# Linear attention into a gated MLP: q loaded in longer runs with kv on both partition halves, and a written order in place of a planner

## The chip, the cores and the metric

One core of a Trainium2 chip. The time is that of one execution on the device in microseconds. A run's time is that of the whole program; the span in a profile goes from the first to the last instruction of the profiled execution. TensorE (PE) multiplies, VectorE (DVE) and ScalarE (ACT) work element by element and empty PSUM, GpSimd (POOL) and SyncE (SP) issue DMAs here. TensorE's operands lie in SBUF, its results in PSUM.

## What is computed

```python
kv  = einsum('bhsd,bhse->bhde', k, v)            # 8 batches, 8 heads, 576 tokens, 64 wide
out = einsum('bhsd,bhde->bhse', q, kv)
x   = out / sqrt(mean(out*out, -1) + 1e-6) * g_norm
x   = x.transpose(0, 2, 1, 3).reshape(4608, 512)  # 4608 tokens, 512 wide
h   = x @ w_in                                    # 512 x 2048
g   = maximum(h, 0) + alpha * minimum(h, 0)
y   = g @ w_out                                   # 2048 x 512, float32 out
```

## The kernel before

Everything is cast to float16 while it is loaded (GpSimd's DMAs cast); PSUM is float32. The 4608 tokens are cut into nine windows `w` of 512. A window goes through three steps, and three windows are under way at a time:

- attention for window `w`: `kv_mm` (name `kv`) makes kv of a batch, 40 matmuls, and `kv_copy` (`kvc`) puts it into `kv_masked` with ScalarE. `rows_mm` (`R.w.1` and `R.w.3`, two token tiles of 128 each) multiplies q, which lies transposed in `qt_sb`, by kv into `or_ps`. Then come squares (`q2`, `q3`), the root (`rs`), the normalisation (`n`, `x_rows`) and a DMA transpose on SyncE into `xt` (`x`).
- the first product: `M.w.u` (and `Ma`) is one block of 128 features, four matmuls, emptied by ScalarE (`r`, `m_sb`) and VectorE (`s`, `gt`). From window 3 on half of it goes by a Strassen-like scheme (`f`, `t`, tiles `mY`, `mV`, `mX`).
- the second product, always by that scheme: `p.w.n.k` is a group of four matmuls into `yX`, `yY`, `yZ`, with sums `S` by VectorE, reads `y` by ScalarE or VectorE, and stores `st`.

q, k and v of batch `b` are loaded two windows ahead by GpSimd (`ld.q.b.t`, `ld.k.b.0`, `ld.v.b.0`; the last 64 tokens apart, as `.4`). k and v come in runs of four tokens of one head, 512 bytes of float16 per partition; 128 partitions times four tokens make the 512 tokens of the main part. From batch 3 on q comes in four loads of 128 tokens, each partition one token of all eight heads, in runs of 64 elements. A DMA transpose (`q.b.t`, line 400) turns each of the four into `qt_sb`. DMA transposes of q and x and some stores (`late`, and `st` of `c12`) share SyncE's queue, which goes in order. A load of k or v must wait until kv of the batch before has been made, a load of q until the old one has been turned. Before each load GpSimd copies one element of `gt` (`gate`, line 1402), which keeps the load from starting early; loads of k and v also copy one element of a transposed tile.

From the second loop on (near 66 us) the order of each engine's work comes from a planner: `AT` holds a due time for each kind of step, and `in_order` takes the due step whose needs are met. The first 66 us have a hand-written order.

Of the kernel before, what the change touches and what calls it, by code (L numbers as in the profile page):

```python
# [17 lines left out]
def kernel(  # L18
# [190 lines left out]
    def load_q(b, t):  # L209
        if (b, "q") not in stages:  # L210
            stages[b, "q"] = stage_for(b, "q", [P, TPP, H, D])
        nc.gpsimd.dma_start(  # L212
            out=stages[b, "q"][:, t, :, :],
            in_=srcs["q"][b, :, t * P : (t + 1) * P, :].rearrange("h p d -> p h d"),
        )
# [176 lines left out]
    def dma_t(b, ts=tuple(range(NT))):  # L392
        qt = qt_sb[b % 2][:, :, PAD : PAD + S]
        for t in ts:
            c0, c1 = t * P, min((t + 1) * P, S)
            if t == TPP:
                src = rem_of(b, "q")[0:REM]
            else:
                src = buf_of(b, "q")[:, t] if b < B_NAT else stages[b, "q"][:, t]
            nc.sync.dma_start_transpose(  # L400
                out=qt[:, :, c0:c1], in_=src.rearrange("p h d -> p (h d)"),
            )
        for j in range(NPAIR):
            qts[b, j] = qt_sb[b % 2][:, j, PAD : PAD + S]

# [99 lines left out]

    def rows_mm(w, tiles):
        o_ps = row_tile([2, 2, NPAIR, D], "or_ps")
        for x, i in enumerate(tiles):
            b, r = divmod(w * W + i * P, S)
            for j in range(NPAIR):  # L510
                if r + P <= S:
                    steps = ((b, PAD + r),)
                else:
                    assert r + PAD == S
                    steps = ((b, S), (b + 1, 0))
                for n, (bb, c) in enumerate(steps):
                    for h in range(2):
                        part = slice(h * D, (h + 1) * D)
                        nc.tensor.matmul(  # L519
                            out=o_ps[:, h, x, j, :],  # L520
                            lhsT=qt_sb[bb % 2][part, j, c : c + P],
                            rhs=kvs[bb, j][part, part],
                            start=(n == 0), stop=(n == len(steps) - 1), skip_group_check=True,
                        )
            ots[w, "r", i] = o_ps[:, :, x]
# [100 lines left out]
    gt_last = []  # L626
    h_turn = [0]
# [72 lines left out]
    def row_pieces(n0):  # L700
        i = 0
        while i < P:
            b, r = divmod(n0 + i, S)
            np_, nt = (P0, T0) if b == 0 else (P, TPP)
            if b < B_NAT and r < np_ * nt:
                t, p = divmod(r, np_)
                cnt = min(P - i, np_ - p)
                yield i, cnt, b, t, p
            else:
                cnt = P - i if b >= B_NAT else min(P - i, S - r)  # L710
                yield i, cnt, None, n0 + i, 0
            i += cnt
# [186 lines left out]
    def quad_out(w, r, h, src, subs=(0, 1)):  # L899
        n0 = w * W + r * HW  # L900
        if n0 >= B_NAT * S and len(subs) == 2:
            put(
                out[n0 : n0 + HW, h * HC : (h + 1) * HC].rearrange("(a p) m -> p a m", p=P),
                src[:],
            )
            return
# [438 lines left out]
    def kv_copy(b):  # L1345
        for i in range(2):
            part = slice(i * D, (i + 1) * D)
            nc.scalar.copy(out=kv_masked[part, b % 4, :, part], in_=kv_tiles[b][part])
# [77 lines left out]
    def load(nm, b):  # L1426
        if nm == "q":
            for t in range(TPP):
                load_q(b, t)
            load_rem(b, "q")  # L1430
        else:
            load_rem(b, nm)
            load_main(b, nm)
# [103 lines left out]
    def put_m2(w):  # L1537
# [17 lines left out]

        full = lambda f, k: f(k) + f(k + 1) if pairs else f(k)
        for k in range(0, 4, 2 if pairs else 1):
            if w > 1:
                sums(3, k, *full(lo, k), *used(7, k))
            sums(1, k, *full(lo, k), *full(hi, k), *used(5, k))  # L1560
            sums(2, k, at(1, k), *used(6, k))
# [105 lines left out]
    def put_rows(w, tiles, free, used):  # L1667
        needs = []
        for i in tiles:
            b, r = divmod(w * W + i * P, S)  # L1670
            needs += [("q", b, t) for t in range(r // P, min((r + P - 1) // P, TPP) + 1)]
            needs.append(("kvc", b))
            if r + P > S:
                needs += [("q", b + 1, 0), ("kvc", b + 1)]
# [16 lines left out]
    def put_moves(w):  # L1691
        b = w + 1
        for t in range(NT if b < B else 0):
            step(("q", b, t), "turn", lambda t=t: dma_t(b, (t,)),
                 (("ld", "q", b, t), *(("R", b - 1, i) for i in (1, 3))))
# [5 lines left out]
    def turned(what, w, i):  # L1701
        if what == "x":
            return xts[w][0:1, 0, i * P : i * P + 1]
        return qt_sb[w % 2][0:1, 0, PAD + i * P : PAD + i * P + 1]
# [7 lines left out]
    def put_load(nm, b):  # L1712
        needs = (("kv", b - 1),) if nm != "q" else ()
        for t in range(NT) if nm == "q" else (TPP, 0):
# [12 lines left out]
            own = (("q", b - 2 if t == TPP else b - 1, t),) if nm == "q" else ()  # L1727
            step(("ld", nm, b, t), "part" if t == TPP else "loadq" if nm == "q" else "load", fn, needs + own + after)

    def put_rest():  # L1730
# [12 lines left out]
        for w in range(min(M1_FROM.values()), NW):  # L1743
            for n in range(1, 5):
# [3 lines left out]
                     (*x_all(w), *((("t", w, n // 2),) if n in (2, 4) else ()), *used))  # L1748
# [24 lines left out]
    for w in range(1, NW):  # L1773
# [3 lines left out]
    LOOP = 27.0  # L1777
    AT = {
# [160 lines left out]
```

## Time and profile before

| | us |
|---|---|
| runs, median of 3 | 273.92 (271.63 to 274.67) |
| the profiled execution | 270.98 |
| its span | 269.2 |
| TensorE busy | 261.9 (97%) |
| VectorE busy | 228.1 (85%) |
| ScalarE busy | 191.8 (71%) |
| GpSimd busy | 94.9 (35%) |

A row of the profile names the line of the kernel, the engine, the operation, and the tiles as written and read (`or_ps<-kv_masked,qt_sb`). Busy time of TensorE contains modelled ends of pipelined matmuls. Engines wait for each other through semaphores; a row's idle time is given with what ended it. "issue" is time in which the profile shows no one to wait for.

### The profile page before, as it was taken

What the parts mean: (1) busy time and instruction counts of PE and PEld (TensorE: products, weight loads), DVE (VectorE), ACT (ScalarE), POOL (GpSimd) and SP (SyncE); (2) the same over time, 40 slices, a digit from 0 to 9 for tenths busy, and PEclk for the clock granted to TensorE, in tenths of its full rate; (3) what the DMA queues carried; (4) which work ended last, traced back from release to release, by engine and by line L of the source; (5) the groups of instructions that cost most, each with busy time, mean ns of one, the idle gap of its engine ahead of it and who ended that gap; (6) DMA issues with size and microseconds to landing.
All of it is one profiled execution on the core that took longest, in us unless ns stands there. A gap on an engine that the chain in (4) does not pass through costs nothing.

```text
span 269.2 us, 6788 instructions
## 1 busy us (share of the span) xinstructions
PE 261.9 (97%) x2477; PEld 182.8 (68%) x2477; DVE 228.1 (85%) x437; ACT 191.8 (71%) x684; POOL 94.9 (35%) x166
## 2 busy tenths in 40 slices
PE   6999999999999999999999999999999999999994
PEld 2554454456556757885788678867885788678883
DVE  6559966899977888999889988998899989978962
ACT  2567637787579779879977997799779983757400
POOL 8853652513530326874346521804040003002100
PEclk9999999999999999999999999999999999999999
DMA  7999999995999899999999993999464013100413
GB/s 189 201 199 206 195 198 189 183 195 92 195 128 169 75 131 126 129 161 197 189 163 156 138 153 66 110 191 129 107 138 99 19 24 119 39 2 11 145 41 118
DMA packets 90821, 35.76 MB, mean 133 GB/s; under 512 B 62996, under 2 KB 88612, under 8 KB 90788
## 3 DMA queue, kind: packets, MB, share of 16 engines
q0 software_dynamic: 57104, 23.68, 68.5%
q1 hardware_dynamic: 32708, 10.63, 24.0%
q10 hardware_dynamic: 976, 1.02, 1.2%
q8 instruction: 19, 0.31, 0.5%
q14 instruction: 14, 0.11, 0.2%
HBM read 36.71 MB, written 9.44 MB: 171 GB/s over the span
## 4 chain that ended last, share of the span: by engine, by line
PE 85%; DMA 8%; ACT 2%; issue 2%; DVE 1%; SPq 1%; POOL 0%; POOLq 0%
PE h_ps L641 23%; PE yY L895 14%; PE yX L895 9%; PE yZ L895 8%; PE mY L1247 8%; PE y L686 5%; PE mV L1247 4%; DMA qt_sb<-qst 3%; PE h_ps L674 2%; DMA vst<-in_v_dram 2%; PE mX L1247 2%; PE or_ps L519 1%; DMA y_sb<-in_g_norm_dram 1%; DMA qst<-in_q_dram 1%; PE kv_ps L1337 1%
## 5 line engine op out<-in xcount | busy, mean ns | idle before, releaser
L641 PE MATMUL h_ps<-xt,w_in_sb 128*128 128x512 f16 x348 | 83.0, 379 | 0.1
L656 DVE SCALAR_TENSOR_TENSOR gt<-m_sb,beta_sb,h_ps 128x512 f16<-128x512 f32 x96 | 67.1, 741 | 4.6 <-ACT m_sb L650 3.6
L650 ACT ACTIVATE m_sb<-h_ps 128x512 f32<-128x512 f32 x96 | 55.0, 604 | 14.3 <-PE h_ps L641 11.9
L641 PEld LDWEIGHTS <-w_in_sb 128*128 128x128 f16 x348 | 33.1, 98 | 32.3 <-issue 0.3
L895 PEld LDWEIGHTS <-s 128*128 128x128 f16 x496 | 48.0, 98 | 8.4 <-DVE s L813 0.2
L895 PEld LDWEIGHTS <-gt 128*128 128x128 f16 x384 | 37.4, 98 | 8.6
L582 ACT ACTIVATE sq_sb<-or_ps 128x64 f16<-128x64 f32 x192 | 39.7, 286 | 2.2 <-PE or_ps L519 2.2
L582 ACT ACTIVATION_READ_ACCUMULATOR sq_sb<-or_ps 128x1 f32 x192 | 39.4, 273 | 0.0
L1402 POOL COPY gate_sb<-gt 1x1 f16<-1x1 f16 x39 | 10.5, 269 | 76.9 <-DVE gt L656 54.7
L895 PE MATMUL yX<-w_out_sb,gt 128*128 128x256 f16 x256 | 35.2, 273 | 0.0
L895 PE MATMUL yY<-wsum,s 128*128 128x256 f16 x256 | 32.9, 273 | 0.0
L698 POOL DMA_DIRECT2D out_dram<-y_sb x24 | 15.2, 639 | 45.8 <-ACT y_sb L957 42.8
L608 DVE TENSOR_TENSOR x_rows<-or_ps,rstd_r 128x512 f16<-128x512 f32 x27 | 17.4, 685 | 9.0 <-ACT rstd_r L592 8.8
L1314 DVE SCALAR_TENSOR_TENSOR gt<-m_sb,beta_sb,mh 128x256 f16<-128x256 f32 x48 | 20.5, 477 | 0.2 <-ACT m_sb L1307 0.2
L1307 ACT ACTIVATE m_sb<-mh 128x512 f32<-128x512 f32 x24 | 15.1, 629 | 6.3 <-DVE mh L1269 6.3
L1266 ACT COPY mu<-mY 128x512 f32<-128x512 f32 x24 | 14.1, 588 | 6.5 <-PE mY L1247 6.5
L1269 DVE TENSOR_TENSOR mh<-mV,mu 128x512 f32<-128x512 f32 x24 | 16.4, 685 | 2.5 <-ACT mu L1266 2.4
L212 POOL DMA_DIRECT2D qst<-in_q_dram x20 | 17.8, 891 | 2.2 <-issue 2.0
L686 PE MATMUL y<-w_out_sb,gt 128*128 128x512 f16 x64 | 16.3, 380 | 0.0
L895 PE MATMUL yZ<-wsum,s 128*128 128x256 f16 x120 | 16.2, 273 | 0.0
L895 PE MATMUL yY<-wsum,gt 128*128 128x256 f16 x128 | 15.5, 273 | 0.0
L1247 PEld LDWEIGHTS <-w_in_sb 128*128 128x128 f16 x144 | 14.1, 98 | 1.6
(150 smaller groups left out, 425.0 us busy)
## 6 DMA issues: line engine op xcount, KB each, us to landing
kst<-in_k_dram POOLq DMA_DIRECT2D x7, 512.0 KB, 7.7
vst<-in_v_dram POOLq DMA_DIRECT2D x6, 512.0 KB, 6.5
out_dram<-y_sb POOLq DMA_DIRECT2D x11, 256.0 KB, 3.2
qst<-in_q_dram POOLq DMA_DIRECT2D x20, 128.0 KB, 4.5
w_out_sb<-in_moe_w_out_dram POOLq DMA_DIRECT2D x8, 256.0 KB, 12.1
out_dram<-y_more POOLq DMA_DIRECT2D x5, 256.0 KB, 4.2
w_in_sb<-in_moe_w_in_dram POOLq DMA_DIRECT2D x2, 512.0 KB, 10.4
qst<-in_q_dram POOLq DMA_DIRECT2D x2, 512.0 KB, 10.7
```

The source lines that it names most:

```text
L212: nc.gpsimd.dma_start(out=stages[b, "q"][:, t, :, :], in_=srcs["q"][b, :, t * P : (t + 1) * P, :].rearrange("h p d -> p h d"),)
L582: nc.scalar.activation(out=sq[:, half, j], in_=o_ps[:, half, j], func=AF.Square, accum_out=ssq[:, half, j : j + 1],)
L608: nc.vector.tensor_tensor(out=xr[:].rearrange("p j h d -> p h j d"), in0=o_ps, in1=rstd[:].unsqueeze(3).to_broadcast([P, 2, NPAIR, D]), op ...
L641: nc.tensor.matmul(out=h_ps[:], lhsT=w_in_blk(c, g), rhs=xts[w][:, c, :], start=(c == 0), stop=(c == NC - 1),)
L650: nc.scalar.activation(out=neg[w, g][:], in_=h_ps[:], func=AF.Relu, scale=-1.0)
L656: nc.vector.scalar_tensor_tensor(out=gts[w, i][:, r, :], in0=neg.pop((w, g))[:], scalar=beta_sb[:, g : g + 1], in1=h_ps[:], op0=ALU.mult, ...
L686: nc.tensor.matmul(out=y[:], lhsT=gt_cols(w, g, a * P, (a + 1) * P), rhs=w_out_blk(g), start=(n == 1), stop=(n == NF),)
L698: engs[store_turn[0] % len(engs)].dma_start(out=dst, in_=src)
L895: nc.tensor.matmul(out=bank, lhsT=lhs, rhs=rhs, start=fresh, stop=(c == NK - 1), skip_group_check=True,)
L1247: nc.tensor.matmul(out=t[bank][:, r, :], lhsT=lhs[:, c, r * P : (r + 1) * P], rhs=rhs[:, c, :], start=(fresh and c == r == 0), stop=(c == ...
L1269: nc.vector.tensor_add(out=h_tile(t, what)[:, :, HW:W], in0=src[:], in1=u[:])
L1314: nc.vector.scalar_tensor_tensor(out=gts[w, i][:, r, cols], in0=m, scalar=beta_sb[:, g : g + 1], in1=h, op0=ALU.mult, op1=ALU.add,)
```

## The change

- From batch 3 on q is loaded like k and v, in two loads of four heads, in 512-byte runs of four tokens. One transpose then holds two heads of all 512 tokens; on its 128 output partitions stand two tokens of a head, 64 partitions each, so a head's tokens lie on either half.
- kv of these batches is therefore kept twice: each head's block lies on both partition halves (one copy of 128x256 and two of 64x256 in place of two of 64x256), and `rows_mm` picks the half by token.
- The tokens of a window stand in another order, with the last 64 of an odd batch first. Tiles that straddle two batches are then made of two pieces of 64 rows, and the output is stored in groups of four tokens.
- The planner is replaced by a list, `ORDER`. `ld.q.5.0@s.3.5` in it is a load that GpSimd gates on the step `s.3.5`; `@!` has no such gate, `@-` the last element made before the list begins.
- Three needs are added for sums whose buffers are read (`read_by`, and one for `t`).

```diff
-    def load_q(b, t):
-        ...
-            out=stages[b, "q"][:, t, :, :],
-            in_=srcs["q"][b, :, t * P : (t + 1) * P, :].rearrange("h p d -> p h d"),
+    QL = 2
+    def load_q(b, i):
+        load_main(b, "q", i * H // QL, (i + 1) * H // QL)
 ...
     def dma_t(b, ts=tuple(range(NT))):
+        for t in ts if b >= B_NAT else ():
+            n = P if t < TPP else REM
+            ...
+                src = stages[b, "q"][:, 2 * t : 2 * t + 2].rearrange("p h t d -> p (h t d)")
+            nc.sync.dma_start_transpose(
+                out=qt_flat(b)[:, t * W : t * W + NC * n].rearrange("p (c n) -> p c n", c=NC),
+                in_=src,
+            )
+    def place_of(b, r):
+        if b >= B_NAT and b % 2:
+            r = r - REM if r >= REM else r + MAIN
+        return divmod(r, P) if r < MAIN else (TPP, r - MAIN)
 ...
+    def row_ops(w, i):
+        ...
+                    half = h if b < B_NAT or t == TPP else t % 2
+                    ...
+                        lhs = qt_flat(b)[part, c : c + n]
+                        rhs = kvs[b][part, half ^ h, j, :]
 ...
     def kv_copy(b):
+        ...
+        nc.scalar.copy(out=kvs[b][:, 0], in_=kv_tiles[b])
         for i in range(2):
-            part = slice(i * D, (i + 1) * D)
-            nc.scalar.copy(out=kv_masked[part, b % 4, :, part], in_=kv_tiles[b][part])
+            part, other = slice(i * D, (i + 1) * D), slice((1 - i) * D, (2 - i) * D)
+            nc.scalar.copy(out=kvs[b][other, 1], in_=kv_tiles[b][part])
 ...
     def put_rows(w, tiles, free, used):
-            needs += [("q", b, t) for t in range(r // P, min((r + P - 1) // P, TPP) + 1)]
+            for b, t, _ in row_parts(w, i):
+                needs += [("q", b, x) for x in ((TPP,) if t == TPP else range(TPP) if b >= B_NAT else (t,))]
 ...
             def fn(t=t, after=after):
-                gate(gt_last[0])
+                for src in load_gate:
+                    gate(src)
 ...
-    LOOP = 27.0
-    AT = {
-        "eyu3": -54736.65, "eyc21": -53910.63, "f2r11": -9714.71, "byu2": -7708.14, "bq23": -7676.19,
-        ...
+    ORDER = """
+        late.2.1 late.2.0 late.2.2 kv.3 M.2.2 S.1.1.0 ld.k.4.4@- S.1.1.1 Ma.2.0 r.2.2 S.1.2.0
+        ...
+        M.2.14 q2.4.0 s.2.15 p.1.3.0 r.2.13 q.4.0 s.2.12 p.2.2.0 ld.q.5.4@s.2.15 q2.4.1 p.2.2.1
+        s.2.13 ld.v.4.4@- p.1.3.1 r.2.14 q.4.3 p.1.3.2 q3.4.1 s.2.14 p.1.3.3 p.2.2.2 q.4.2 S.2.1.1
+        rs.4.1 p.2.2.3 q3.4.0 S.2.3.1 Ma.3.0 y.1.c12 q.4.1 M.3.0 M.3.1 S.2.2.0 y.2.seed r.3.0 n.4.1
+        M.3.2 ld.q.5.1@s.2.12 rs.4.0 S.2.4.0 r.3.1 x.4.1 M.3.3 y.2.c11 n.4.0 st.1.c21 r.3.2 t.3.1
+        p.2.6.0 x.4.0 S.2.2.1 kv.4 S.2.3.0 p.2.6.1 kvc.4 s.3.0 p.2.6.2 p.2.6.3 t.3.2 s.3.2 M.3.4
+        y.2.u2 ld.k.5.0@! s.3.1 r.3.3 R.4.3 r.3.4 M.3.6 s.3.3 q2.4.2 s.3.4 M.3.7 st.1.c11 r.3.6
+        ...
+        f.3.3.s22 f.3.3.4 y.3.p1 Ma.4.0 f.3.3.r21 f.3.3.c12 q.5.0 p.2.3.0 f.3.3.s21 f.3.3.r12 M.4.1
+        q3.5.0 st.1.c12 S.3.1.0 M.4.2 q3.5.1 S.3.2.0 p.2.3.1 f.3.3.s12 rs.5.0 p.3.2.0 rs.5.1 p.3.2.1
+        t.4.1 p.2.3.2 t.4.3 n.5.1 M.4.0 p.2.3.3 r.4.0 n.5.0 M.4.3 x.5.1 r.4.1 s.4.0 r.4.2 kv.5 s.4.1
+        ld.q.6.1@s.4.0 x.5.0 M.4.4 s.4.2 kvc.5 st.1.c22 y.2.c12 M.4.5 r.4.4 S.3.1.1 M.4.6 y.3.seed
+        ld.v.6.4@! s.4.4 r.4.5 ld.q.6.0@f.3.2.s12 S.3.2.1 p.3.6.0 r.4.3 f.4.2.1 r.4.6 p.3.6.1
+        st.2.c21 s.4.6 p.3.6.2 st.2.c11 p.3.6.3 t.4.2 f.4.2.seed s.4.3 R.5.3 y.3.u2 f.4.2.2 s.4.5
+        ...
+    """.split()
     def in_order():
-        ...
+        todo = {".".join(map(str, s[0])): s for s in steps if s[1]}
+        ...
+            if at:
+                load_gate[:] = [gates[at]] if at != "!" else []
+            yield s[2]
```

More of the change, by code (lines that the diff above doesn't have):

```diff
@@ L504, in xt_cols, with row_parts @@
         return xts[w][:, j, :]
+    def row_parts(w, i):
+        n0 = w * W + i * P
+        out, x = [], 0
+        while x < P:
+            b, r = divmod(n0 + x, S)
+            t, p = place_of(b, r)
+            n = min(P - x, REM if t == TPP else P)
+            out.append((b, t, slice(x, x + n)))
+            assert p == 0 or b < B_NAT
+            x += n
+        return out
+    def row_ops(w, i):
+        ops = []
+        for b, t, rows in row_parts(w, i):
+            for j in range(NPAIR):
+                for h in range(2):
+                    n = rows.stop - rows.start
+                    half = h if b < B_NAT or t == TPP else t % 2
+                    part = slice(half * D, (half + 1) * D)
+                    if b < B_NAT:
+                        r = w * W + i * P + rows.start - b * S
+                        lhs = qt_sb[b % 2][part, j, PAD + r : PAD + r + n]
+                        rhs = kvs[b, j][part, part]
+                    else:
+                        c = (
+                            TPP * W + j * REM if t == TPP
+                            else (2 * j + h) * 2 * P + t // 2 * P
+                        )
+                        lhs = qt_flat(b)[part, c : c + n]
+                        rhs = kvs[b][part, half ^ h, j, :]
+                    ops.append((half, h, rows, j, lhs, rhs))
+        return ops
@@ L506, in rows_mm @@
     def rows_mm(w, tiles):
         o_ps = row_tile([2, 2, NPAIR, D], "or_ps")
+        ops = [row_ops(w, i) for i in tiles]
+        apart = all(len({y[0] for y in x}) == 1 for x in ops)
+        left = []
         for x, i in enumerate(tiles):
[L509 to L524, printed above, removed]
@@ L525, in rows_mm @@
-            ots[w, "r", i] = o_ps[:, :, x]
+            half = ops[x][0][0]
+            ots[w, "r", i] = o_ps[:, half] if apart else o_ps[:, :, x]
+            left += [(x, *op) for op in ops[x]]
+        if not apart:
+            left.sort(key=lambda y: y[3].stop - y[3].start)
+        was = None
+        while left:
+            n = next((n for n, y in enumerate(left) if was and y[1] != was[1]), 0)
+            x, half, h, rows, j, lhs, rhs = was = left.pop(n)
+            nc.tensor.matmul(
+                out=ots[w, "r", tiles[x]][rows, h, j, :], lhsT=lhs, rhs=rhs, start=True,
+                stop=True, skip_group_check=True,
+            )
@@ L626 @@
     gt_last = []
+    load_gate = []
     h_turn = [0]
@@ L1345, in kv_copy @@
     def kv_copy(b):
+        if b < B_NAT:
+            for i in range(2):
+                part = slice(i * D, (i + 1) * D)
+                nc.scalar.copy(out=kv_masked[part, b % 4, :, part], in_=kv_tiles[b][part])
+            return
+        kvs[b] = kv_masked[:, b % 4].rearrange("p j (x d) -> p x j d", x=2)
+        nc.scalar.copy(out=kvs[b][:, 0], in_=kv_tiles[b])
         for i in range(2):
-            part = slice(i * D, (i + 1) * D)
-            nc.scalar.copy(out=kv_masked[part, b % 4, :, part], in_=kv_tiles[b][part])
+            part, other = slice(i * D, (i + 1) * D), slice((1 - i) * D, (2 - i) * D)
+            nc.scalar.copy(out=kvs[b][other, 1], in_=kv_tiles[b][part])
     def row_kv(bs):
@@ L1427, in load @@
         if nm == "q":
-            for t in range(TPP):
-                load_q(b, t)
+            for i in range(QL):
+                load_q(b, i)
             load_rem(b, "q")
@@ L1559, in put_m2 @@
                 sums(3, k, *full(lo, k), *used(7, k))
-            sums(1, k, *full(lo, k), *full(hi, k), *used(5, k))
-            sums(2, k, at(1, k), *used(6, k))
+            sums(1, k, *full(lo, k), *full(hi, k), *used(5, k), *read_by(2, k))
+            sums(2, k, at(1, k), *used(6, k), *read_by(4, k))
             sums(4, k, at(2, k), *used(3, k))
@@ L1703, in turned @@
             return xts[w][0:1, 0, i * P : i * P + 1]
-        return qt_sb[w % 2][0:1, 0, PAD + i * P : PAD + i * P + 1]
+        return qt_flat(w)[0:1, i * W : i * W + 1]
     def turns_before(nm, b):
@@ L1726, in fn @@
                     load_main(b, nm)
-            own = (("q", b - 2 if t == TPP else b - 1, t),) if nm == "q" else ()
+            own = ()
+            if nm == "q":
+                n = TPP // QL
+                own = (("q", b - 2, t),) if t == TPP else tuple(("q", b - 1, n * t + i) for i in range(n))
             step(("ld", nm, b, t), "part" if t == TPP else "loadq" if nm == "q" else "load", fn, needs + own + after)
```

188 lines of the change are left out of this document (106 added, 82 removed), and 65 rows, old and new, of the table AT.

## The prediction

> **What bounds the kernel now.** I read the page first, then the chain that ended last, then busy time in stretches, and last the stretches in which TensorE was not full. The page:
>
> ```profile
> span 269.2 us, 6788 instructions
> PE 261.9 (97%) x2477; PEld 182.8 (68%) x2477; DVE 228.1 (85%) x437; ACT 191.8 (71%) x684; POOL 94.9 (35%) x166
> q0 software_dynamic: 57104, 23.68, 68.5%
> PE 85%; DMA 8%; ACT 2%; issue 2%; DVE 1%; SPq 1%; POOL 0%; POOLq 0%
> ```
>
> TensorE is busy 97% of the span and holds 85% of the chain. DMA holds 8%, though, and a busy PE includes modelled pipeline ends, so the question is where TensorE is short of work. The stretches after the part that the change leaves alone (it begins near 66 us, with the second loop):
>
> ```profile
> core 0: us, PE busy (x) PEld busy (x) DVE busy (x) ACT busy (x) POOL busy (x), PEclk, DMA share, GB/s
> 66.00:80.00 14.00, 13.71 (x138) 7.86 (x137) 12.78 (x28) 9.37 (x34) 7.27 (x14) 1.00 1.42 160
> 95.00:110.00 15.00, 14.80 (x155) 10.33 (x154) 12.43 (x21) 12.89 (x59) 6.86 (x15) 1.00 1.29 132
> 125.00:140.00 15.00, 14.45 (x170) 11.26 (x170) 12.73 (x24) 12.63 (x53) 6.94 (x13) 1.00 1.40 156
> 140.00:165.00 25.00, 25.00 (x260) 19.00 (x258) 22.79 (x43) 21.64 (x96) 10.78 (x20) 1.00 1.17 151
> 190.00:215.00 25.00, 25.00 (x228) 19.17 (x226) 23.84 (x45) 21.74 (x95) 3.35 (x5) 1.00 0.39 82
> ```
>
> The first number after the comma is PE's busy time. It misses 14.00 - 13.71 = 0.29 us, 15.00 - 14.80 = 0.20 and 15.00 - 14.45 = 0.55: 1.04 us together. From 140 us on it misses nothing. The clock is 1.00 throughout. The DMA engines are oversubscribed (a share over 1 means packets that overlap) in just those stretches that have a gap. The chain there, from two stretches (start, length, what):
>
> ```profile
> 72.98 4.52 DMA qt_sb<-qst
> 78.14 5.48 DMA vst<-in_v_dram
> 92.90 3.90 DMA qst<-in_q_dram
> 96.83 4.35 DMA qt_sb<-qst
> 101.22 0.41 PE or_ps L519 x16
> ...
> 125.04 0.75 PE kv_ps L1337 x40
> 125.80 1.83 PE h_ps L641 x8
> 127.63 0.55 issue
> 128.17 0.53 PE or_ps L519 x24
> ```
>
> All three gaps stand before `or_ps`, the product of q with kv. The first two end with a transpose of q landing. The third is put down to "issue", but the transposes of q that SyncE issued just before tell who it was:
>
> ```profile
> 117.64 1.19 SPq L400 DMA_TRANSPOSE qt_sb<-qst  x1
> 118.88 1.62 SPq L400 DMA_TRANSPOSE qt_sb<-qsb  x1
> 120.59 2.02 SPq L400 DMA_TRANSPOSE qt_sb<-qst  x1
> ...
> DMA to landing us min/median/max: 6.9/7.5/8.7
> ...
> DMA to landing us min/median/max: 2.3/4.3/8.7
> ```
>
> The first landing line is for the transposes of 117 to 130 us alone, the second for all 30. 120.59 + 7.5 = 128.1, and `or_ps` starts at 128.17. So what TensorE lacks in this stage is q, 1.04 us of it in this execution.
>
> **The change part by part.** *q's loads.* From batch 3 on, 20 loads of 128 KB become 10 of 256 KB, in runs four times as long. The price of the old and of the new form stands in the trace, since k is loaded in the new form already:
>
> ```profile
> kst<-in_k_dram POOLq DMA_DIRECT2D x7, 512.0 KB, 7.7
> qst<-in_q_dram POOLq DMA_DIRECT2D x20, 128.0 KB, 4.5
> L212 POOL DMA_DIRECT2D qst<-in_q_dram x20 | 17.8, 891 | 2.2 <-issue 2.0
> L1402 POOL COPY gate_sb<-gt 1x1 f16<-1x1 f16 x39 | 10.5, 269 | 76.9 <-DVE gt L656 54.7 <-DVE gt L1314 22.2
> L698 POOL DMA_DIRECT2D out_dram<-y_sb x24 | 15.2, 639 | 45.8 <-ACT y_sb L957 42.8 <-DVE y_sb L963 3.0
> ```
>
> A batch of q costs 4 x 4.5 = 18.0 us of landings one after the other against 7.7 for a like amount of k; two halves of 256 KB lie between. On GpSimd's queue ten issues of 0.891 us go (8.9 us), 20 of the 39 gate copies at 0.269 (5.4 us), and ten more stores come at 0.639 (6.4 us), as output rows now lie in groups of four tokens: 7.9 us less in all. GpSimd is busy 35%, so this is off the path; if its queue were full it would be 7.9 us of earlier loads. What is on the path is when the transposes land.
>
> *The waits at `or_ps`.* The 0.55 us goes: the written order puts the five transposes of batch 5 one right behind the other on SyncE, and between the last (`q.5.0`) and their first reader `R.5.3` stand eleven groups of 0.44 us, seven of `M` (six of 0.86, one of 0.22) and `kv.5`'s 0.75, by the rows further down: 11 us, more than the 8.7 of the longest landing. The 0.20 us goes too, as I take it: `R.4.1` now reads batch 3 alone, and `R.4.3` has 6.2 us of cover (worked out below) against the 4.3 of the median. The 0.29 us I leave in: the first transposes of batch 3 still queue on SyncE behind six stores that nothing moves:
>
> ```profile
> 67.26 5.61 SPq L698 DMA_DIRECT2D out_dram<-y_sb  x6
> 72.98 5.15 SPq L400 DMA_TRANSPOSE qt_sb<-qst  x4
> ```
>
> Sum of this part: -0.75 us; bounds -1.04 (all three go) and +2.5 (`R.4.3`, rivals).
>
> *kv on both halves.* Two copies of 64x256 per batch become one of 128x256 and two of 64x256, for five batches:
>
> ```profile
> L1348 ACT CAST kv_masked<-kv_ps 64x256 f16<-64x256 f32 x12 | 4.3, 361 | 0.2 <-PE kv_ps L1337 0.2
> L387 ACT COPY qt_sb<-qt_ps 128x256 f16<-128x256 f16 x1 | 0.4, 405 | 0.0
> ```
>
> The nearest row for the added copy is 0.405 us: 5 x 0.405 = 2.0 us of ScalarE, which is 71% busy. It counts only where `or_ps` waits for it. The shortest way in the new order is from `kv.4` to `R.4.3`: three groups of 0.44 us and one of 0.86 lie between, 2.2 us, against 0.405 + 2 x 0.361 = 1.1 us of copies. That hides them, so I take nothing; bounds 0 and 2.0.
>
> *The products.* `or_ps` keeps 240 matmuls, all 64 columns wide; 48 of them now write 64 rows instead of adding a zero-padded half into 128. Rows for it: 24 took 0.53 us above, and the narrow kv form 40 in 0.75, so 22 and 19 ns each: 48 x 3 ns is under 0.2 us either way. I take nothing.
>
> ```profile
> 125.60 0.20 PE L1337 MATMUL kv_ps<-vsb,ksb 128*64 128x64 f16 x2
> 125.73 1.90 PE L641 MATMUL h_ps<-xt,w_in_sb 128*128 128x512 f16 x8
> ```
>
> The trace shows a switch from 64-column to 128-column work with no idle time: one row begins before the other has ended. [...]
>
> *The order.* A planner's due times give way to a written list, so every engine's order changes from 66 us on. Twelve of GpSimd's loads lose their gate and start as soon as its queue reaches them; SyncE's stores of `c12` still stand in its queue between transposes, now at other places. TensorE has the same number of instructions. As TensorE misses nothing from 140 us on, the new order can gain next to nothing there; it can lose. VectorE is the reason: 23.84 of 25.00 us busy at 190 to 215, 1.16 us free. No row prices another order, so its bounds are 0 and a loss of one window's free time in each of five windows (5 x 1.16 = 5.8); I take 0, the nearer row being the stretches without a gap.
>
> *Runs against the profiled execution.* That one took 270.98 us, 1.78 around the span of 269.2. The runs took 271.63 to 274.67, median 273.92: 2.94 above it. On its own the sum gives 270.98 - 0.75 = 270.2. What makes the runs longer isn't in the trace. If it is later landings of q at these same three places (the landing times vary from 2.3 to 8.7 us), the change takes it away; if it lies in the first 66 us, where weights load, it stays. I take two thirds, 2.0 us, since the stage with gaps and full DMA engines is the one the change works on: 273.92 - 0.75 - 2.0 = 271.2. The bounds are 273.2 (nothing of it) and 270.2 (all).
>
> **The rivals.** *Nothing moves:* TensorE has the same 2477 matmuls and was short by 1.04 of 269.2 us; the runs' excess is in the untouched beginning. For it: the gapless stretches from 140 us. Against: at the three places a later landing passes to the end in full, and landings vary by 6.4 us. 273.92 - 0.75 = 273.2.
>
> *All of the excess goes:* lighter DMA traffic makes each run like the profiled one and closes all three gaps, 270.98 - 1.04 = 269.9, and a little less where modelled ends hide short waits. For it: gaps and oversubscribed DMA coincide. Against: k and v, 512 KB each, stay and cross the transposes as before.
>
> *All heads at once (slower):* a transpose now carries two heads for all tokens, where it carried all heads for 128 tokens. The first product of a batch must await all four. `R.4.3` decides. After `q.4.1`, the last, the list has `M.3.0` to `M.3.4` (0.22 + 4 x 0.86), `p.2.6.0` to `p.2.6.3` (4 x 0.44) and `kv.4` (0.75) ahead of it, from these rows and the 0.75 above:
>
> ```profile
> 121.14 0.86 PE h_ps L641 x4
> 123.74 0.44 PE yX L895 x4
> ```
>
> That is 6.2 us of cover. A landing of 6.9 to 8.7 us, as at 117 to 130, stalls it by 0.7 to 2.5. Behind it wait `x` of window 4 and TensorE's whole queue. Price with the small 64 KB load of v that also moved up against `kv.4` late by the same amount: 273.92 + 2 x 2.5 - 0.55 = 278.4 at the worst, 276 in the middle. Against: only small loads are in flight then.
>
> *VectorE becomes the bound (slower):* the list lets sums and normalisations come in another order; if its new waits use up the free 1.16 us in each of five windows and exceed it by as much again, TensorE waits for the excess: 273.92 + 5.8 - 0.75 = 279.0; with two thirds of that, 277.0. It decides where VectorE's free time, 5% at 190 to 215 us, is used up. Against: the same instructions, spread more evenly over the list.
>
> **How the numbers follow.** Forecast, two thirds of the excess and two of three gaps: 0.46, its own range 270.2 to 273.2. Nothing moves: 0.12. All of it goes: 0.17. All heads at once: 0.12. VectorE: 0.13. One per cent is 2.7 us, about what a measurement of this kernel can tell from no change, so the limits are 271.2 and 276.7. Half of the forecast lies under 271.2 (0.23); with the 0.17 that is 0.40 faster. Of the slower rivals two thirds of the first (0.08) and nearly all of the second (0.12) pass 276.7: 0.20. The rest is 0.40. The range, 268.6 to 276.8, leaves out most of the two slower rivals' ends and no more than 2 in 10.
>
> **What the changed profile would show.** Right: loads of q landing in about 5 us for 256 KB; the chain between 70 and 130 us without `qt_sb<-qst`; no gap before the `or_ps` near 128 us; PE's missing time in 66 to 140 us under 0.5 us; the page's q0 share well under 68.5%. Wrong: an idle row at `or_ps` near 101 us ended by a transpose, or at `kv_ps` ended by `vsb` (all heads); PE busy under 24.9 of 25 us after 140 with VectorE at 24 or more (VectorE). The forecast is wrong outright if the gaps are gone and the median is still above 273.2.

## The result, and the profile after

| | us |
|---|---|
| the kernel before, median of 22 runs | 272.33 (271.39 to 275.12) |
| the changed kernel, median of 22 runs | 271.38 (270.00 to 275.42) |
| ratio of the changed to the kernel before | 0.9951 (95%: 0.9927 to 0.9974) |
| profiled execution, changed kernel | 271.0, span 269.1 |
| profiled execution, kernel before | 270.98, span 269.2 |

The change is worth half a per cent, 0.95 us between the medians, and 271.38 is within 0.2 us of the forecast. In two later sets of runs, beside other kernels, the changed kernel came out at 0.9975 (0.9946 to 1.0004) and 0.9961 (0.9923 to 0.9998) of the kernel before; the first of these intervals does not exclude that nothing changed. The two profiled executions, though, are equally long, so the profile must show something given for something taken. (Ratios are over undisturbed runs and medians over all of them; of the kernels below, the profiled executions of the layout with the planner and of the three moves were disturbed ones, so the first is read only for what waits on what and the second not at all.)

The page of the changed kernel, with the same rows as shown of before:

```profile
span 269.1 us, 6703 instructions
...
PE 262.0 (97%) x2477; PEld 183.1 (68%) x2477; DVE 225.7 (84%) x437; ACT 192.3 (71%) x689; POOL 85.1 (32%) x146
...
q0 software_dynamic: 41744, 23.68, 63.7%
...
PE 87%; DMA 4%; DVE 4%; ACT 2%; SPq 1%; issue 1%; DVEq 0%
```

DMA's share of the chain has halved, from 8% to 4%. VectorE's has grown from 1% to 4%. GpSimd is busy 9.8 us less. The same bytes go in 41744 packets instead of 57104. The large loads don't land sooner for that: by the two pages' lists of DMA issues a load of k takes 8.3 us in place of 7.7, and one of v 8.4 in place of 6.5. The stretches:

```profile
66.00:80.00 14.00, 14.00 (x150) 8.97 (x149) 11.07 (x24) 8.87 (x32) 4.79 (x10) 1.00 1.04 156
80.00:95.00 15.00, 14.36 (x128) 9.72 (x126) 9.82 (x17) 13.66 (x88) 3.37 (x8) 1.00 1.26 153
95.00:110.00 15.00, 15.00 (x156) 10.16 (x154) 13.65 (x25) 12.69 (x61) 8.29 (x17) 1.00 1.18 143
...
125.00:140.00 15.00, 15.00 (x170) 11.18 (x168) 12.79 (x21) 13.04 (x54) 7.77 (x13) 1.00 0.98 161
...
165.00:190.00 25.00, 24.48 (x260) 18.48 (x259) 22.97 (x44) 21.07 (x92) 6.25 (x10) 1.00 1.02 162
```

The three old stretches with a gap (66 to 80, 95 to 110, 125 to 140) are full: all 1.04 us are back. But 0.64 us are missing at 80 to 95 and 0.52 at 165 to 190, 1.16 us together, where nothing was missing before. Old gaps closed, new ones opened, and the sum is the same. The chain through the first new stretch (start, length, what) names two causes:

```profile
77.62 6.91 DMA qt_sb<-qst
...
84.58 0.31 PE or_ps L567 x8
...
90.08 0.68 DVE s L856
90.76 0.61 DVE x_rows L653
...
91.42 0.41 PE or_ps L567 x16
```

At 84.58 `R.3.3` waits for the last transpose of batch 3 (`q.3.2`), issued at 77.62 and 6.91 us under way. At 91.42 `R.4.1` waits for the PSUM tile that VectorE's normalisation `n.3.3` (`x_rows`) empties, and VectorE took a sum, `s` of line 856, 0.68 us, first. What was in flight beside that transpose shows GpSimd's queue in the same stretch:

```profile
76.58 0.44 POOL L1448 COPY gate_sb<-qt_sb 1x1 f16<-1x1 f16 x1 [5.93 <-DMA qt_sb<-qst]
77.13 0.88 POOL L204 DMA_DIRECT2D vst<-in_v_dram  x1
...
78.36 0.88 POOL L204 DMA_DIRECT2D kst<-in_k_dram  x1
```

The gate lets v and k of batch 4 (512 KB each) go as soon as the *first* transpose has landed. Four of the five transposes were issued before v's load; the fifth came 0.5 us after it, and landed at 84.53, when v's load did (77.13, and 7.5 us to landing by the list of DMA issues). Such a transpose behind a large load is called a crossing below. The third new gap, 0.52 us at 180 us, stands before `kv.7`:

```profile
180.43 0.32 PE L1376 MATMUL kv_ps<-vst,kst 128*64 128x64 f16 x8 [0.52 <-DVE gt L702]
```

The profile puts it down to VectorE's `gt`, which ended at 180.41. But v of batch 7 landed within 0.1 us of that: its load went out at 171.03, after GpSimd's queue had sat behind a store until 169.49, and took 9.3 us. In this execution either of the two would have made the gap alone.

### The profile page after: what moved, and what is told of

It reads as the page before. It is cut to its first block, busy times and chain, and to the rows that moved or that the text cites. A ratio compares the mean times of both kernels' runs of the same rounds, so it can differ in the third digit from the quotient of the medians.

```text
span 269.1 us, 6703 instructions
## 1 busy us (share of the span) xinstructions
PE 262.0 (97%) x2477; PEld 183.1 (68%) x2477; DVE 225.7 (84%) x437; ACT 192.3 (71%) x689; POOL 85.1 (32%) x146
## 3 DMA queue, kind: packets, MB, share of 16 engines
q0 software_dynamic: 41744, 23.68, 63.7%
## 4 chain that ended last, share of the span: by engine, by line
PE 87%; DMA 4%; DVE 4%; ACT 2%; SPq 1%; issue 1%; DVEq 0%
PE h_ps L687 25%; PE yY L940 15%; PE yX L940 9%; PE yZ L940 9%; PE mY L1286 8%; PE y L732 5%; PE mV L1286 4%; DMA qt_sb<-qst 3%; PE mX L1286 2%; PE h_ps L720 2%; PE or_ps L567 2%; PE kv_ps L1376 2%; DMA y_sb<-in_g_norm_dram 1%; ACT sq_sb L627 1%; DVE gt L1353 1%; PE ssq_ps L492 1%
## 5 line engine op out<-in xcount | busy, mean ns | idle before, releaser
L687 PE MATMUL h_ps<-xt,w_in_sb 128*128 128x512 f16 x348 | 84.0, 379 | 0.0
L702 DVE SCALAR_TENSOR_TENSOR gt<-m_sb,beta_sb,h_ps 128x512 f16<-128x512 f32 x96 | 68.5, 744 | 12.3 <-ACT m_sb L696 11.5
L687 PEld LDWEIGHTS <-w_in_sb 128*128 128x128 f16 x348 | 33.0, 98 | 31.2 <-issue 0.3
L627 ACT ACTIVATE sq_sb<-or_ps 128x64 f16<-128x64 f32 x192 | 40.8, 261 | 1.6 <-PE or_ps L567 1.1
L940 PE MATMUL yX<-w_out_sb,gt 128*128 128x256 f16 x256 | 36.8, 273 | 0.0
L744 POOL DMA_DIRECT2D out_dram<-y_sb x31 | 18.3, 597 | 26.7 <-ACT y_sb L996 16.2
L744 POOL DMA_DIRECT2D out_dram<-y_more x11 | 6.6, 601 | 50.7 <-DVE y_more L1002 30.6
L1448 POOL COPY gate_sb<-gt 1x1 f16<-1x1 f16 x19 | 4.1, 216 | 47.8 <-DVE gt L702 37.4
L940 PE MATMUL yY<-wsum,gt 128*128 128x256 f16 x128 | 16.6, 272 | 0.0
L940 PE MATMUL yZ<-w_out_sb,s 128*128 128x256 f16 x120 | 16.0, 273 | 0.0
## 6 DMA issues: line engine op xcount, KB each, us to landing
w_out_sb<-in_moe_w_out_dram POOLq DMA_DIRECT2D x8, 256.0 KB, 12.2
```

Source lines behind the costliest of these rows:

```text
L627: nc.scalar.activation(out=sq[:, half, j], in_=o_ps[:, half, j], func=AF.Square, accum_out=ssq[:, half, j : j + 1],)
L687: nc.tensor.matmul(out=h_ps[:], lhsT=w_in_blk(c, g), rhs=xts[w][:, c, :], start=(c == 0), stop=(c == NC - 1),)
L702: nc.vector.scalar_tensor_tensor(out=gts[w, i][:, r, :], in0=neg.pop((w, g))[:], scalar=beta_sb[:, g : g + 1], in1=h_ps[:], op0=ALU.mult, ...
L744: engs[store_turn[0] % len(engs)].dma_start(out=dst, in_=src)
L940: nc.tensor.matmul(out=bank, lhsT=lhs, rhs=rhs, start=fresh, stop=(c == NK - 1), skip_group_check=True,)
```

## The experiments

**The changed kernel again, twice.** Do the gaps belong to the order, or to one execution?

> The changed kernel again, beside three others on one chip. By its first runs (271.38 us against 272.33, fast runs 0.995) it should come out at 271 to 272 us and 0.994 to 0.998 of the kernel before. Its profile is a second draw: theory A (the gaps are made by the order and the loads that cross the transposes) expects the same three new gaps again, at or_ps near 84 us, at or_ps near 91 us and at kv_ps near 180 us, within 0.3 us of 0.44, 0.53 and 0.69 each; theory B (gaps are drawn anew in each execution, wherever a transfer happens to land late) expects at least one of them to be absent and another place to show one.

> The changed kernel a third time, as the neighbour of three others on the same chip: 271 to 272 us, 0.995 to 0.998 of the kernel before. Of its gaps the one at or_ps near 91 us, VectorE's, should be there again (0.53, 0.54 and 0.55 us so far in it and in the kernel with four loads), the one near 84 us between 0.3 and 1.7 us, and the one at kv_ps near 180 us in some executions only.

Measured: 271.55 and 271.77 us. TensorE's waits from 66 us to 262 (us in total, times, longest), in the first repetition:

```profile
PE or_ps L567 <- DMA qt_sb<-qst: 0.5, 1, 0.5
PE or_ps L567 <- DVE x_rows L653: 0.4, 1, 0.4
```

and in the second:

```profile
PE kv_ps L1376 <- DMA vst<-in_v_dram: 0.6, 1, 0.6
PE h_ps L687 <- DMA xt<-x_rows: 0.5, 1, 0.5
PE or_ps L567 <- DVE x_rows L653: 0.4, 1, 0.4
PE or_ps L567 <- DMA qt_sb<-qst: 0.3, 1, 0.3
```

Both theories have a share. VectorE's gap is there in all three and as long in each; that it is the list's, a later experiment shows. That of the transpose is there in all three and varies. That at `kv_ps` comes in two of three, and in the second repetition it is v's load that ends it. Gaps over three executions: 1.16, 0.90 and 1.73 us. The expectations give each single gap some 0.16 us longer than the profile's waits (0.44, 0.53 and 0.69 for 0.28, 0.37 and 0.52): they count from the end of the group before on the chain (0.44 us long), the waits from the end of its row (0.60), which contains the modelled end of the pipeline.

**One half of the change at a time.** The new layout with the old planner:

```diff
-                for src in load_gate:
-                    gate(src)
+                gate(gt_last[0])
...
-    ORDER = """ ... """.split()
+    AT = { ... }   # and in_order of the kernel before
```

> The new layout of q and the doubled kv, with the planner of the kernel before instead of the written list, and its gates. Theory 1 (the gain is q's longer runs and the lighter DMA traffic): about 271.4 us, ratio 0.995, the three old gaps smaller or gone, q0 share near 64%. Theory 2 (the gain is the written order; the layout alone moves nothing or loses through copies and narrow products): 272.3 to 273.3 us, ratio 1.000 to 1.004, with the gaps of 0.29, 0.20 and 0.55 us at or_ps still there since the transposes stand behind the same stores. My prediction gave 0.75 us to both together; the 0.55 us gap it put down to the new order of the transposes, the 0.20 us to fewer batches per reader, so by it this kernel shows the 0.55 still and comes out near 272.1.

Measured: 289.38 us, 1.062 of the kernel before (95%: 1.0572 to 1.0669; the figures below are written the same way). Neither theory had this. Its waits, and the one on the chain at 77 us:

```profile
PE or_ps L567 <- DMA qt_sb<-qst: 8.4, 4, 6.6
PE or_ps L567 <- DMA qt_sb<-qsb: 5.2, 4, 3.6
```

```profile
77.25 4.44 DMA qt_sb<-qsb
...
81.73 0.54 PE or_ps L567 x16
```

In the new layout the first tile of an odd batch is its 64-token rest (`qsb`), and every later tile of the batch needs all four transposes. The planner's due times were set for the old layout: with them the rest of batch 3 is turned last, at 77.25 us, and near 165 us the fourth transpose of a batch goes out at 168.42, behind three stores and two transposes of x. So TensorE stands for 3.6 us at the start of batch 3 and for 6.6 us from 165.5 us on, 13.6 us in all at transposes of q. The written list turns the rest second. Due times set for the new layout were not tried.

And the written list with the old layout:

```diff
-    def load_q(b, i):   # two halves of 256 KB
+    def load_q(b, t):   # four loads of 128 KB, as before; old dma_t, rows_mm, kv_copy
...
-    ... R.7.3 ... q.7.0 ...
+    ... q.7.0 R.7.3 ...
```

> The written order with q's old layout, four loads of 128 KB a batch (each half load of the list becomes two of them at its place) and the old kv copies. One entry is moved: the first transpose of batch 7 stands ahead of R.7.3, which reads it in the old layout. Theory 2 (the order is the gain): about 271.4 us, ratio 0.995. Theory 1 (the layout is the gain): 272.3 us or more, ratio 1.000, q0 share near 68.5%. Both expect the gap at or_ps near 91 us, which comes from VectorE's order (0.5 us), and the one at kv_ps near 180 us, which comes from GpSimd's queue (0.7 us). If the loads of k and v that cross the transposes of batch 3 make the gap near 84 us, it is here too, 0.3 us or more, since the old transposes cost the same bytes.

Measured: 281.25 us, 1.0367 (1.0317 to 1.0418). Again neither. Two waits make it:

```profile
PE or_ps L519 <- DMA qt_sb<-qst: 9.0, 2, 4.9
```

The first is the crossing again, only worse. The rest of q landed later, behind more loads (its transpose started at 75.29, in the changed kernel at 73.78), v's load went out at 77.38, and the *two* last transposes fell behind it, at 77.86 and 79.17, instead of one:

```profile
79.17 9.53 DMA qt_sb<-qst
...
88.74 0.61 PE or_ps L519 x16
```

The second stands behind stores on SyncE, where the list has `q.7.0` too late for a layout in which `R.7.3` reads it. Its profiled span is 281.2 us, 12.0 over that of before. 9.0 us of it are these waits (4.9 and 4.1); for the rest see the last section.

The same kernel, mended at both places: k and v of batch 4 behind `q.3.2`, and `q.7.0` ahead of the stores. (Its expectation gives the two waits of 4.9 and 4.1 us as 5.1 and 4.3, counted on the chain as said above.)

> The written order with q's old layout once more (it took 281.25 us, with two stalls at or_ps of 5.1 and 4.3 us), now with the loads of k and v for batch 4 behind the last transpose of batch 3, and the first transpose of batch 7 eight entries further ahead, in front of the stores of the fourth window that SyncE waited for. If the list alone makes the order good and the layout is indifferent, both stalls go and it takes 270.5 to 272 us, as the changed kernel does or better. If the layout itself is needed (four loads of 128 KB on GpSimd's queue and readers that need the next batch's first tile), stalls of 0.5 us and more remain at other or_ps and the time is over 272.5 us. The clock, granted at 0.77 in the 15 us with the first stall, should be back at 1.0 where the stall is gone.

Measured: 275.10 us, 1.0088 (1.0046 to 1.0129). The wait of 4.9 us is gone. That of 4.1 has become one of 1.8 before the same `R.7.3`. The clock is 1.00 in all stretches from 66 to 262 us. The waits that are left:

```profile
PE or_ps L519 <- DMA qt_sb<-qst: 1.8, 1, 1.8
PE h_ps L675 <- DMA xt<-x_rows: 1.3, 2, 0.8
PE or_ps L519 <- DVE x_rows L608: 0.6, 1, 0.6
```

The 1.8 us, on the chain:

```profile
175.85 6.36 DMA qst<-in_q_dram
182.23 4.92 DMA qt_sb<-qst
187.20 0.49 PE or_ps L519 x22
```

The stores no longer stand ahead of `q.7.0`; now the load of q that it turns is late.

So the two halves of the change are not a sum: by the ratios, on 272 us, the layout alone costs 17 us and the list alone 10 (mended, 2.4), and both together gain 1.3. This list is bad for the old layout, and these due times are bad for the new one. Whether a list written for the old layout would match the planner's own 272 us wasn't tried, so it isn't shown that the old layout can't be served as well.

**Four loads instead of two.**

```diff
-    QL = 2
+    QL = 4   # in ORDER: ld.q.b.0 -> ld.q.b.0 ld.q.b.1, ld.q.b.1 -> ld.q.b.2 ld.q.b.3
```

> The changed kernel with q of a batch in four loads of 128 KB (two heads each, still in runs of 512 bytes) instead of two of 256 KB; nothing else differs. If the length of the runs is what lightens the DMA engines, the q0 share stays at 63 to 65% and the packets near 75460, a load lands in 4 us or less where the old one took 4.5, and the time is that of the changed kernel within 0.2%. If the number of loads counts, the share goes back towards 68.5% and the time to 272.3 us. GpSimd issues ten more loads, 8.9 us by 0.891, on a queue that is 32% busy: nothing by the prediction.

Measured: 271.70 us, 1.0007 (0.9982 to 1.0031), where the changed kernel beside it had 271.55.

```profile
DMA packets 75620, 35.75 MB, mean 132 GB/s; under 512 B 42676, under 2 KB 73412, under 8 KB 75588
...
q0 software_dynamic: 41904, 23.68, 64.3%
```

The packets and the share stay down (41904 and 64.3% on q0, against 41744 and 63.7% with two loads and 57104 and 68.5% in the kernel before): in these runs it is the 512-byte run that lightens the DMA engines, not the number of loads. A load of 128 KB took 4.9 us, not the 4 or less expected. In its profile `R.3.3` waited 1.5 us for `q.3.2`, and the medians differ by 0.15 us; the intervals don't separate the two.

**Closing the new gaps.** First the crossing: k and v of batch 4 wait for the last transpose of batch 3.

```diff
-        return (("q", 3, 0) if b == 4 else ("x", b - 1, 1),)
+        return (("q", 3, 2) if b == 4 else ("x", b - 1, 1),)
...
-    ... ld.v.4.0@s.2.2 ... ld.k.4.0@s.2.0 q.3.2 ...
+    ... q.3.2 ld.v.4.0@s.2.2 ld.k.4.0@s.2.0 ...
```

> The changed kernel with the two 512 KB loads of k and v for batch 4 moved behind the last transpose of batch 3 (q.3.2) in the list, and gated on that transpose's landing instead of the first one's. Theory A (a transpose that is issued behind such a load lands only when the load does: 84.53 against 84.58 us in the changed kernel, 88.69 against 89.58 in the old layout with the list): q.3.2 lands within 3 us of its issue, the gap at or_ps near 84 us (0.44, 0.69 and 1.71 us in three executions of this order) goes, and the time falls by 0.5 to 1.0 us, 270.7 us. Theory B (the landing is slow for another reason, such as the stores ahead of it on SyncE): the gap stays within 0.3 us of what it was and the time is the same. Later k and v cost nothing by both, since kv.4 reads them 40 us later.

Measured: 271.36 us, 0.9973 (0.9941 to 1.0004). Theory A was right on the mechanism. The landing times of the transposes of q in 71 to 92 us (of the three of five for which the profile has one), in the changed kernel:

```profile
DMA to landing us min/median/max: 2.5/2.5/6.9
```

and in this one:

```profile
DMA to landing us min/median/max: 2.4/2.5/2.5
```

It was wrong on the time, because the loads now cross the next transposes on SyncE, those of x, and TensorE waits for these. Their landing times in 82 to 93 us (2.6 to 5.5 us in the changed kernel), and the chain:

```profile
DMA to landing us min/median/max: 7.0/9.0/9.3
```

```profile
89.62 7.01 DMA xt<-x_rows
...
96.77 1.03 PE h_ps L720 x8
```

The wait came back as one of 0.7 us at `h_ps`. The two loads of q for batch 4, issued behind k's, were slowed too: 11.1 and 12.2 us to landing in place of 5.4 and 5.8. So this move chose other transposes and loads for the crossing and did not end it.

Second, VectorE's order:

```diff
-    ... S.2.1.0 rs.3.3 r.2.15 n.3.3 ...
+    ... rs.3.3 r.2.15 n.3.3 S.2.1.0 ...
```

> The changed kernel with one entry of the list moved: VectorE's sum S.2.1.0 stands behind the normalisation n.3.3 instead of two places ahead of it. If the gap at or_ps near 91 us (0.53, 0.54 and 0.55 us in three executions) is VectorE's order, it goes, and the time falls by 0.5 us, about 0.2%; the sum is 0.68 us long. If n.3.3 is held by something else (its rstd from ScalarE), the gap stays. The gap near 84 us stays in both cases.

> The changed kernel with S.2.1.0 behind n.3.3 once more, on one chip with the changed kernel, since its 270.66 us (0.9953 of the kernel before) and the changed kernel's 271.4 to 271.55 came from different calls. If the gap of 0.53 us at or_ps is worth its length, it is 0.4 to 0.7 us below the changed kernel here; if something else takes it up, the two are within 0.2 us.

Measured: 270.66 us, 0.9953 (0.9925 to 0.9982), and beside the changed kernel 271.06 us, 0.9954 (0.9923 to 0.9986), against its 271.77 and 0.9961. VectorE's queue in the first of them, where line 653 (`n.3.3`) now stands ahead of line 856:

```profile
90.63 0.68 DVE L653 TENSOR_TENSOR x_rows<-or_ps,rstd_r 128x512 f16<-128x512 f32 x1
91.23 0.68 DVE L856 TENSOR_TENSOR s<-gt 128x1024 f16<-128x1024 f16 x1
```

Its only wait of TensorE between 66 and 262 us is the transpose:

```profile
PE or_ps L567 <- DMA qt_sb<-qst: 0.4, 1, 0.4
```

The gap is gone in both executions, so it was made by the list's order on VectorE, and no other wait of its length took its place. Both spans are 268.8 us; the changed kernel's three are 269.1, 268.8 and 269.9. This version is faster than the kernel before by 0.5%, with intervals below 1 both times; against the changed kernel the medians say 0.7 us, but the ratios overlap, so that part isn't shown.

Third, the loads of batch 7 ahead of a store on GpSimd's queue, alone and with the two others:

```diff
-    ... st.4.c21 ... ld.k.7.4@! ... ld.v.7.0@! ...
+    ... ld.k.7.4@! ld.v.7.0@! st.4.c21 ...
```

> The changed kernel with only the third move: the two loads of k and v for batch 7 ahead of the store st.4.c21 on GpSimd's queue. The three moves together brought nothing (272.03 us, fast runs 0.999 of before, where -1.2 to -1.7 us was expected); the first alone brought nothing (271.36), the second alone 0.7 us. If this move is the one that loses, by putting 512 KB of v next to 512 KB of k and across the transposes of x near 165 us, it is slower here: 272 us or more. If the loss is in the first and second together, this one is at 271 to 271.5 us, with no gap at kv_ps near 180 us.

> Three moves together: the loads of k and v for batch 4 behind the last transpose of batch 3, S.2.1.0 behind n.3.3, and the two loads of k and v for batch 7 (ld.k.7.4, ld.v.7.0) ahead of the store st.4.c21 that held them on GpSimd's queue from 164 to 169 us. The gaps they aim at were 0.44, 0.53 and 0.69 us in the profile of the changed kernel, 0.69, 0.54 and none in its second one. So 1.2 to 1.7 us less than the changed kernel, 270.0 us in the median, ratio 0.992 to the kernel before, with TensorE short of nothing between 66 and 262 us. If the gaps only move to the next late thing, the time is that of the changed kernel, 271.5 us.

Measured: alone 271.37 us, 0.9954 (0.9921 to 0.9987); all three 272.03 us, 0.9992 (0.9959 to 1.0026). Alone it does no harm and no gap stands at `kv_ps`, but that gap comes in some executions only, so one profile doesn't prove that the move closed it. All three together missed the expected 270.0: their interval leaves out the 0.992 that was forecast. So the forecast sum of the three did not come. That something is lost when they are together isn't shown, as the intervals of this kernel and of the single moves overlap; why the sum did not come is open.

**The cost of the extra copy.**

```diff
         nc.scalar.copy(out=kvs[b][:, 0], in_=kv_tiles[b])
+        nc.scalar.copy(out=kvs[b][:, 0], in_=kv_tiles[b])
```

> The changed kernel with the new 128x256 copy of kv done twice for each of the batches 3 to 7 (the second writes the same values to the same place). My prediction cost the new copy at 0.405 us and at nothing in time, as hidden between kv and the first or_ps of the batch. If so, five more of them, 2.0 us of ScalarE, move the median by less than 0.3 us. If ScalarE's order matters, up to 2.0 us more, 273.4 us.

Measured: 272.23 us, 1.0005 (0.9973 to 1.0037), beside the changed kernel's 271.77 and 0.9961 (0.9923 to 0.9998). The medians differ by 0.46 us, between "hidden" (under 0.3) and "in full" (2.0), the ratios by 0.0044 or 1.2 us, and the intervals overlap. In its profile no wait of TensorE from 66 to 262 us is ended by ScalarE. That speaks for a copy that is hidden for the most part; the times alone don't settle it.

## Why the prediction was right in its number and wrong in its working

*Closing the gaps, -0.75 us.* The places and the mechanism were right: the gap near 128 us and the one near 101 went, as forecast. The 0.29 us at 77 us that I left in went too, since I looked at SyncE's queue and not at the new reader: the straddling tile now reads only the 64-token rest of batch 3, which the list turns second. What the step missed is that the changed kernel has gaps of its own: 1.16 us in place of 1.04. In the profile this term measured +0.12 - 1.16 opened less 1.04 closed - and not -0.75; over three executions the new gaps averaged 1.26 us. One reading ahead of this step was wrong as well: DMA shares over 1 do not stand in just the stretches with a gap. The prediction's own table has 1.17 at 140 to 165 us with none, and the stretches left out of it, 80 to 95 and 110 to 125, have 1.13 and 1.28 with none. A share over 1 alone makes no gap here; it takes a transfer that a reader is waiting for.

*Runs against the profiled execution, -2.0 us.* This step failed. I read 2.94 us between the median of three runs and the profile as late landings, two thirds of which would go. Most of it was the draw: over 22 runs the kernel before has 272.33 us, and 272.07, 272.16 and 272.40 in three later sets. Its excess is 1.35 us, not 2.94; in the changed kernel 271.38 - 271.0 = 0.38. So about 1.0 us went, half of what I took, from a start 1.6 us too high. Even that 1.0 hangs on which executions were profiled: in the two repetitions the changed kernel's excess is 0.87 and 0.00 us. Together I took off 2.75 us from 273.92, and the runs showed 0.95 off 272.33: the two errors cancel, and the number is right by luck. Where that 0.95 us lies, no profile shows, as the only one of before is of an execution 1.35 us below its median.

*kv on both halves, 0.* Bounds held, as far as the runs can tell. ScalarE is busy 192.3 us after 191.8, and doubling the copy moved the median by 0.46 of 2.0 us.

*The products, 0 and "under 0.2 us either way".* Mis-sized. A group of 24 with straddling tiles stands at 0.46 us on the chain of the kernel before and at 0.60 in the changed one:

```profile
182.42 0.46 PE or_ps L519 x24
```

```profile
184.39 0.60 PE or_ps L567 x24
```

There are three such groups. The busy time of `or_ps` from 66 to 262 us (first number after the comma), before and after:

```profile
66.00:262.00 196.00, 5.41 (x216) 15.46 (x24) 40.75 (x384) 1.00 0.85 116
```

```profile
66.00:262.00 196.00, 5.76 (x216) 16.27 (x24) 44.28 (x384) 1.00 0.79 116
```

That is 0.35 us more, but waits blur it: before, the first of the three groups is cut in two by its wait (0.69 us busy, 0.56 after), and in the changed kernel `R.3.3`, which has no narrow products, is cut by its own (0.58 in place of 0.41). The two groups that are whole in both went from 0.53 to 0.68 and from 0.52 to 0.68. Three times that is 0.46 us, an estimate, where I had taken 0. Whether the narrow form itself costs it, or the switch to it, the trace doesn't tell.

*The order, 0 with bounds 0 and +5.8.* Its own new gap is VectorE's, a wait of 0.37 us or 0.53 on the chain, shown by moving one entry; VectorE is not the bound that the rival spoke of (23.41 of 25 us at 190 to 215, less than before). But to cost the order by itself was the wrong question. The layout without it costs 17 us, and it without the layout 10. My expectation for the layout with the planner, 272.1, came from adding parts, and missed by 17 us.

*GpSimd, off the path.* Right: 9.8 us less against the 7.9 worked out, and ten more loads were worth no more than the runs can tell.

*All heads at once.* The rival's mechanism is real; I placed it wrongly. `R.4.3` had the cover I counted. `R.3.3`, which I didn't price, waits for all four transposes of batch 3, by 0.3 to 0.5 us here. With the planner 8.4 of the 13.6 us of waits are of this kind; the other 5.2 are at the 64-token rest.

*The signs.* Right: loads of 256 KB landing in 5.6 us, no gap near 128, q0 at 63.7%. Wrong: the chain from 70 to 130 us has a `qt_sb<-qst`, and PE misses 0.64 us between 66 and 140, above the 0.5 allowed.

## What to carry to other kernels

A change of layout changes who needs which transfer first, so price it together with the order in which transfers are issued: here an order made for one layout lost 10 to 17 us with the other. A load gated on the first of several transposes goes out ahead of the last of them; look for what is issued just after a large load (here that transpose took 6.91 us to land in place of 2.5), and expect a moved load to cross something else (here the transposes of x, 7.0 to 9.3 us in place of 2.6 to 5.5). With one profile and three runs, the distance between them is a draw and no term of a sum.

## What the runs showed of the hardware

In the old layout with the list two stalls of TensorE, of 4.9 and 4.1 us, cost more than their length. Its granted clock (the number ahead of the last two) around the first of them, which ends at 88.7 us:

```profile
80.00:83.00 3.00, 3.00 (x25) 2.32 (x24) 0.67 (x1) 2.97 (x21) 0.18 (x1) 1.00 1.22 149
83.00:88.00 5.00, 0.82 (x4) 0.20 (x2) 2.09 (x4) 1.57 (x3) 0.00 (x0) 0.88 1.56 131
88.00:91.00 3.00, 2.26 (x21) 1.06 (x22) 0.00 (x0) 1.61 (x16) 1.31 (x3) 0.50 0.95 143
91.00:94.00 3.00, 3.00 (x17) 2.17 (x16) 1.61 (x3) 2.66 (x20) 2.52 (x5) 0.57 1.30 85
94.00:97.00 3.00, 3.00 (x18) 1.57 (x16) 2.10 (x5) 1.49 (x4) 0.00 (x0) 1.00 1.66 136
```

The clock falls to half (0.88 over 83 to 88, 0.50 over 88 to 91) and is back at 1.00 from 94 on, after about 5 us of work. The same four matmuls on the chain, at once behind the stall and later:

```profile
89.35 1.82 PE h_ps L642 x4
...
94.17 0.86 PE h_ps L642 x4
```

A mean of 0.57 from 91 to 94 is half the clock for 2.6 us of these three, so it lasted from 88.7 to about 93.6. Of these 4.9 us half are lost, 2.4 us, half of the stall's own length again (an estimate from these rows). The second stall, of 4.1 us, does it again (the work resumes at 194.05):

```profile
194.00:197.00 3.00, 2.95 (x29) 1.64 (x30) 0.00 (x0) 1.25 (x9) 0.00 (x0) 0.50 0.53 106
197.00:200.00 3.00, 3.00 (x15) 1.83 (x14) 2.66 (x5) 2.08 (x11) 1.44 (x2) 0.60 0.35 104
```

Worked out the same way it lasts to 199.4 and loses 2.7 us. The waits and the two losses make 14.1 us, an estimate, where the 12.0 us of longer span and the 1.04 us of gaps that this kernel hasn't got make 13.0; so the clock covers the rest, and the estimate is some 1 us too high. In the mended kernel a stall of 1.8 us left the clock at 1.00; what a stall between 1.8 and 4.1 us does, these rows don't show.

In the changed kernel a DMA transpose issued just behind a 512 KB load landed with it, at 84.53 us against 84.6 (77.13 + 7.5): 6.91 us after its issue (7.24 in the kernel with `S.2.1.0` behind `n.3.3`), against 2.5 for those ahead of it. The last one in the old layout with the list took 9.53 us and landed at 88.69; k's load, issued at 78.73, landed 10.8 us later, at 89.5. The transposes of x took 7.0 to 9.3 us once they crossed the loads. With the loads issued after it, the last transpose of batch 3 took 2.5 us. Why such a transpose lands no sooner, no run here shows.
